# A four-layer attention kernel: sums one step behind the scores, PSUM laid out per stage, and the first query chunk started early

## The chip, the cores and the metric

The kernel runs on one core of one Trainium2 chip. The metric is device time in microseconds (us) of one execution. The kernel before takes 5196.6 us, the median of two runs that lie between 5195.6 and 5197.61. "Granted clock" is the share of full TensorE clock that the chip allowed in a stretch of time.

## The reference, cut to what matters

There are four layers, A, B, A, B, on one sequence of 2048 tokens with 1024 features and 32 heads of 32. Both kinds add their result to x.

```python
def _A_ref(x, wqkv, w_phi, wo):                    # linear attention
    ...
    phi_q = concat([softmax(q @ w_phi), softmax(-(q @ w_phi))])   # features of queries
    phi_k = concat([softmax(k @ w_phi), softmax(-(k @ w_phi))])   # features of keys
    kv  = einsum("bhsf,bhsd->bhfd", phi_k, v)      # needs every key first
    z   = einsum("bhsf->bhf", phi_k)
    o   = (phi_q @ kv) / (phi_q @ z + 1e-6)
    return o @ wo

def _B_ref(x, wqkv, wo):                           # full attention
    ...
    p = softmax((q @ k.T) * Dh ** -0.5)
    return (p @ v) @ wo

x = x + _A_ref(_layernorm(x), A_wqkv, A_w_phi, A_wo)
x = x + _B_ref(_layernorm(x), B_wqkv, B_wo)
x = x + _A_ref(_layernorm(x), A_wqkv, A_w_phi, A_wo)
x = x + _B_ref(_layernorm(x), B_wqkv, B_wo)
```

Layer B has 32 x 2048 x 2048 scores, and each needs an exponential. Layer A has an obstacle in it: no query can be finished before all keys have been summed.

## The kernel before

Tokens are handled in four chunks of 512. The stages follow each other in this order. The first stage makes normalisation, values and key features of the first layer A. Then, twice: the projections to B (query features of A, its output projection, normalisation, keys and values of B, and B's queries for the first chunk), and the attention of B. The code calls the first pair of layers A and B "layer 0" and the second pair "layer 1", and so does this text.

Attention runs in steps, 1,024 in all. One step takes one group of four heads, 256 queries and 256 keys. It has 8 score matmuls, packed four at a time by rows of the array, two exponentials of 128x1024, and 16 sum matmuls, packed four at a time by columns. Half of the sums are with the values and half with ones, which gives the softmax denominators.

```python
def step(self, q, kv, g, half, kc, begin, end, acc, oT, first, last):
    n = 3 if mode[0] == "narrow" else 2
    ...  # two score tiles of two PSUM banks each, from a ring of n
    for k in range(2):
        for j in range(4):
            ...
            PE.matmul(tiles[j // 2][:, o:o + QH], lhsT=kv[rows, 0, ...],      # L496
                      rhs=q[rows, g, ...], start=True, stop=True,
                      tile_position=(32 * j, 0), skip_group_check=True)
    for i in range(2):
        e = T("E", [P, 2, 2, QH], BF16)
        SC.activation(out=e[:], in_=tiles[i][:]..., func=ACT.Exp, scale=SCALE)  # L505
        es.append(e)
    self.lag = (kv, g, half, kc, begin, end, acc, oT, first, last, es)

def finish(self):
    if self.lag is None:
        return
    kv, g, half, kc, begin, end, acc, oT, first, last, es = self.lag
    self.lag = None
    if begin:
        self.nd = psum.tile([P, C], F32, tag="ND", ...)       # one bank for the sums
    ...
                PE.matmul(nd[rows, part * QH:(part + 1) * QH],                # L527
                          lhsT=ones_bf[:, 0:32] if part else kv[:, 1, col:col + 32],
                          rhs=es[j // 2][:, j % 2, i, :], ...)
    ...  # at the end of a group: copy or add nd to acc, or divide into oT
```

Other work (projections of the next queries, output projection of the chunk before) is a generator; it is dealt out in pieces between a step's scores and its sums:

```python
for _ in b:                    # one attention step: scores and exponentials
    got = 0.0
    while alive and got < per:
        u, end = next(bg)      # one piece of background work, usually 8 matmuls
        got += u
        if end:
            break
    att.finish()               # the sums of the same step
```

PSUM has 8 banks of 2 KiB per partition (the Trainium skill, "PSUM — Partial Sum Buffer", Specifications; the layouts of both kernels are built to that number). The kernel before holds three two-bank tiles for scores, one bank for sums (ND) and one for background work (BG). When no attention runs, projections use the two-bank tiles, cut in two:

```python
t = psum.tile([P, 2 * C], F32, tag=f"S{2 - k}", name=f"wide{serial[0]}")
halves.extend([t[:, 0:C], t[:, C:2 * C]])
```

The softmax here doesn't subtract the row's maximum and nothing guards it: scores larger than these inputs give would overflow.

## Time and profile before

The stages are read from the timeline, from the first matmul of one to the first of the next:

| stage | us |
|---|---|
| first stage | 396 |
| layer 0, projections of the first chunk / of the three others | 144 / 386 |
| layer 0, attention of four query chunks | 1,779 |
| layer 0, last output projection and the next layer's keys | 105 |
| layer 1, projections | 530 |
| layer 1, attention | 1,816 |
| tail | 40 |

Attention is about 3,590 of 5,197 us. The page of the kernel before gives the whole-span shares of the engines, the granted clock in 40 slices in tenths, and the chain of work that ended last:

```profile
PE 3167.5 (61%) x29982; PEld 1346.2 (26%) x30208; DVE 1326.9 (26%) x1808; ACT 2160.7 (42%) x2353; POOL 276.9 (5%) x218
...
PEclk9777787755696588578557877855585567556555
...
PE 45%; ACT 21%; issue 18%; DVE 7%; POOL 1%; DMA 0%; another core or an unknown queue 0%; ACTq 0%; POOLq 0%; DVEq 0%; SPq 0%
```

No engine is near full, and the clock falls to half in the attention stages. The windows view of the kernel before shows two stretches of attention, one without and one with background work:

```profile
core 0: us, PE busy (x) PEld busy (x) DVE busy (x) ACT busy (x) POOL busy (x), PEclk, DMA share, GB/s
1100.00:1300.00 200.00, 108.33 (x1318) 45.22 (x1308) 17.91 (x19) 104.76 (x109) 0.00 (x0) 0.50 0.05 17
940.00:970.00 30.00, 20.92 (x275) 9.39 (x280) 6.33 (x8) 19.38 (x20) 0.00 (x0) 1.00 0.20 71
```

Without background work PE is busy 108 of 200 us and ACT 105 of 200, at a clock of 0.50. With background work the clock is 1.00, and the step takes 3.03 us instead of 3.67. Two engines at about half, neither of them waiting for anything else, are the picture of a serial loop: each works while the other waits. The timeline of the kernel before shows the loop (columns: start, length, engine, line, operation, tiles, shape, and in brackets the idle time before it and what ended it):

```profile
983.72 1.02 ACT L505 ACTIVATE E_4820<-s_4810 128x1024 bf16<-128x1024 f32 x1 [1.73 <-PE s_4811 L496]
984.64 1.02 ACT L505 ACTIVATE E_4822<-s_4811 128x1024 bf16<-128x1024 f32 x1
984.80 0.40 PE L527 MATMUL nd_4763<-E_4820,kv_4177 128*32 128x256 bf16 x2 [1.17 <-ACT E_4820 L505]
985.71 0.40 PE L527 MATMUL nd_4763<-E_4822,kv_4177 128*32 128x256 bf16 x2 [0.52 <-ACT E_4822 L505]
...
986.88 0.42 PE L496 MATMUL s_4841<-q_2496,kv_4177 32*128 32x256 bf16 x2
987.39 1.02 ACT L505 ACTIVATE E_4850<-s_4840 128x1024 bf16<-128x1024 f32 x1 [1.73 <-PE s_4841 L496]
```

ACT starts the pair of exponentials at 983.72 and the next pair at 987.39: 3.67 us a step, of which it waits 1.73 for scores. PE waits 1.17 and 0.52 us for the exponentials. The sums wait for the exponentials of their own step, and the program has the next scores behind those sums: the lines show PE take them up in this order, the last sums at 985.71 and the next scores at 986.88.

The second thing to see is in the projections. The timeline of the kernel before, PE, in an output projection, one line for one group of 8 matmuls of 512 columns:

```profile
594.53 3.18 PE L156 MATMUL wide_2800<-c_531_2728,w_2640 128*128 128x512 bf16 x8
598.49 1.89 PE L156 MATMUL wide_2800<-c_531_2728,w_2640 128*128 128x512 bf16 x8 [0.78 <-DVE x_1968 L408]
600.21 1.89 PE L156 MATMUL bg_2819<-c_531_2728,w_2640 128*128 128x512 bf16 x8
```

Two groups share the tile "wide_2800", one in each half. The second waits until DVE has emptied the first half, although it writes the other bank.

### The profile page before, as it was taken

What the parts mean: (1) busy time and instruction counts of PE and PEld (TensorE: products, weight loads), DVE (VectorE), ACT (ScalarE), POOL (GpSimd) and SP (SyncE); (2) the same over time, 40 slices, a digit from 0 to 9 for tenths busy, and PEclk for the clock granted to TensorE, in tenths of its full rate; (3) what the DMA queues carried; (4) which work ended last, traced back from release to release, by engine and by line L of the source; (5) the groups of instructions that cost most, each with busy time, mean ns of one, the idle gap of its engine ahead of it and who ended that gap; (6) DMA issues with size and microseconds to landing.
All of it is one profiled execution on the core that took longest, in us unless ns stands there. A gap on an engine that the chain in (4) does not pass through costs nothing.

```text
span 5197.0 us, 68008 instructions
## 1 busy us (share of the span) xinstructions
PE 3167.5 (61%) x29982; PEld 1346.2 (26%) x30208; DVE 1326.9 (26%) x1808; ACT 2160.7 (42%) x2353; POOL 276.9 (5%) x218
## 2 busy tenths in 40 slices
PE   4656666655676577567555766755565566556555
PEld 2232222222232233223222222222222222222222
DVE  3454444100123023123115444310021011111101
ACT  1010000455566566556541000155565555555553
POOL 1221000000000000000001000000000000000000
PEclk9777787755696588578557877855585567556555
DMA  5223333200021021011002333400011001000000
GB/s 156 93 77 122 113 120 119 94 17 17 25 94 41 17 84 50 25 60 50 25 12 90 123 117 117 138 28 22 17 54 45 17 25 54 29 17 25 26 17 9
DMA packets 221416, 309.59 MB, mean 60 GB/s; under 512 B 41920, under 2 KB 189376, under 8 KB 213440
## 3 DMA queue, kind: packets, MB, share of 16 engines
q1 hardware_dynamic: 221120, 305.23, 17.8%
q8 instruction: 236, 3.87, 0.3%
q14 instruction: 60, 0.49, 0.0%
HBM read 236.52 MB, written 60.29 MB: 57 GB/s over the span
## 4 chain that ended last, share of the span: by engine, by line
PE 45%; ACT 21%; issue 18%; DVE 7%; POOL 1%; DMA 0%; another core or an unknown queue 0%; ACTq 0%; POOLq 0%; DVEq 0%; SPq 0%
PE nd_7976 L527 0%; PE nd_28185 L527 0%; PE nd_36665 L527 0%; PE nd_12464 L527 0%; PE nd_39829 L527 0%; PE nd_40078 L527 0%; PE nd_26208 L527 0%; PE nd_6989 L527 0%; PE nd_40816 L527 0%; PE nd_20937 L527 0%; PE nd_19701 L527 0%; PE nd_15758 L527 0%; PE nd_39088 L527 0%; PE nd_38322 L527 0%; PE nd_36173 L527 0%
## 5 line engine op out<-in xcount | busy, mean ns | idle before, releaser
L527 PEld LDWEIGHTS <-ones 128*32 128x32 bf16 x8192 | 417.8, 118 | 24.7
L183 PEld LDWEIGHTS <-ones 128*128 128x128 bf16 x128 | 12.9, 103 | 168.6 <-issue 167.2
L379 PEld LDWEIGHTS <-Rsel 128*128 128x128 bf16 x128 | 17.0, 133 | 143.7 <-issue 143.7
L179 POOL TENSOR_TENSOR sq_9474<-c_1591_9471 128x512 bf16<-128x512 bf16 x1 | 1.4, 1354 | 606.5 <-DVE c_1591_9471 L173 606.5
L188 ACT ACTIVATE f_3978<-wide_3945,eps 128x512 f32<-128x512 f32 x1 | 0.7, 687 | 71.1 <-PE wide_3945 L183 71.1
L188 ACT ACTIVATE f_23660<-wide_23616,eps 128x512 f32<-128x512 f32 x1 | 0.7, 687 | 69.6 <-PE wide_23616 L183 69.6
L188 ACT ACTIVATE f_23132<-bg_23099,eps 128x512 f32<-128x512 f32 x1 | 0.7, 687 | 69.5 <-PE bg_23099 L183 69.5
L188 ACT ACTIVATE f_24187<-wide_24154,eps 128x512 f32<-128x512 f32 x1 | 0.7, 687 | 69.5 <-PE wide_24154 L183 69.5
L188 ACT ACTIVATE f_22524<-wide_22480,eps 128x512 f32<-128x512 f32 x1 | 0.7, 687 | 69.3 <-PE wide_22480 L183 69.3
L188 ACT ACTIVATE f_2923<-bg_2890,eps 128x512 f32<-128x512 f32 x1 | 0.7, 687 | 69.2 <-PE bg_2890 L183 69.2
L188 ACT ACTIVATE f_3451<-wide_3407,eps 128x512 f32<-128x512 f32 x1 | 0.7, 687 | 68.5 <-PE wide_3407 L183 68.5
L188 ACT ACTIVATE f_2315<-wide_2271,eps 128x512 f32<-128x512 f32 x1 | 0.7, 687 | 67.9 <-PE wide_2271 L183 67.9
L344 ACT ACTIVATE ea_22805<-f_22803 128x512 bf16<-128x512 f32 x2 | 1.1, 620 | 58.2 <-DVE f_22803 L341 58.2
L344 ACT ACTIVATE ea_2596<-f_2594 128x512 bf16<-128x512 f32 x2 | 1.1, 621 | 57.5 <-DVE f_2594 L341 57.5
L156 PEld LDWEIGHTS <-c_109_666 128*128 128x128 bf16 x128 | 14.0, 110 | 38.7 <-issue 28.5
L156 PEld LDWEIGHTS <-c_266_1434 128*128 128x128 bf16 x128 | 13.7, 107 | 36.4 <-issue 25.4
L156 PEld LDWEIGHTS <-c_34_316 128*128 128x128 bf16 x128 | 14.2, 111 | 34.2 <-issue 24.2
L156 PEld LDWEIGHTS <-c_3416_21758 128*128 128x128 bf16 x128 | 13.3, 104 | 32.9 <-issue 21.1
L156 PEld LDWEIGHTS <-c_188_1054 128*128 128x128 bf16 x128 | 13.1, 104 | 32.5 <-issue 20.2
L344 ACT ACTIVATE ea_3124<-f_3122 128x512 bf16<-128x512 f32 x2 | 1.1, 620 | 42.2 <-DVE f_3122 L341 42.2
L505 ACT ACTIVATE E_4173<-s_4163 128x1024 bf16<-128x1024 f32 x1 | 1.0, 1023 | 41.4 <-PE s_4163 L496 41.4
L527 PEld LDWEIGHTS <-kv_7235 128*32 128x32 bf16 x128 | 8.2, 116 | 38.5 <-issue 37.3
(11593 smaller groups left out, 10645.7 us busy)
## 6 DMA issues: line engine op xcount, KB each, us to landing
w_301<-in_A_wqkv_dram SPq DMA_DIRECT2D x1, 1024.0 KB, 7.2
w_303<-in_A_wqkv_dram SPq DMA_DIRECT2D x1, 1024.0 KB, 8.4
x_d_72<-x_162 SPq DMA_DIRECT2D x1, 1024.0 KB, 4.2
x_d_73<-x_291 SPq DMA_DIRECT2D x1, 1024.0 KB, 4.5
w_404<-wpk_d SPq DMA_DIRECT2D x1, 1024.0 KB, 6.5
xa_d_76<-c_34_316 SPq DMA_DIRECT2D x1, 1024.0 KB, 3.8
w_444<-wpk_d SPq DMA_DIRECT2D x1, 1024.0 KB, 6.6
w_651<-in_A_wqkv_dram SPq DMA_DIRECT2D x1, 1024.0 KB, 6.6
```

Of the source, the lines that this page charges most:

```text
L156: PE.matmul(ps, lhsT=lhsT(po), rhs=rhs(po), start=(po == 0), stop=(po == G - 1))
L179: (DVE if fast and po % 2 else POOL).tensor_tensor(out=sq[:], in0=xc[:, po, :], in1=xc[:, po, :], op=ALU.mult)
L183: PE.matmul(ps, lhsT=ones_bf[:], rhs=sq[:], start=(po == 0), stop=(po == G - 1))
L188: SC.activation(out=lnv[:], in_=ps, func=ACT.Ln, scale=1.0 / D, bias=eps_t[:])
L344: SC.activation(out=e[:, s, :], in_=pq[:], func=ACT.Exp, scale=1.0 - 2.0 * s)
L379: PE.matmul(ps, lhsT=Rsel[:, g, s, :], rhs=ab[:], start=True, stop=True)
L505: SC.activation(out=e[:], in_=tiles[i][:].rearrange("p (j k q) -> p j k q", k=2, q=QH), func=ACT.Exp, scale=SCALE,)
L527: PE.matmul(nd[rows, part * QH:(part + 1) * QH], lhsT=ones_bf[:, 0:32] if part else kv[:, 1, col:col + 32], rhs=es[j // 2][:, j % 2, i, :] ...
```

## The change

The change has four parts.

1. The sums run one step behind. Scores and exponentials of step n+1 are issued before the sums of step n.
2. PSUM is laid out anew per stage: 8 single banks for projections alone ("wide"); 2 score tiles, 3 background banks and ND in a middle stage ("mid"); 3 score tiles, one background bank and ND in the rest of attention ("narrow"). No projection uses half of a two-bank tile.
3. The first query chunk attends to each key chunk as soon as that is made, beside the projections of the next chunk. Its partial sums wait in SBUF (`acc`).
4. In the first stage ACT takes squares and evictions, exponentials of key features read PSUM directly, POOL no longer squares, and the normalisation of the next chunk is dealt between the projections of this one.

The diff, cut to its core:

```diff
-        w=4, c8=3, x=2, q=2, kv=2, st=2, E=5, ea=8, acc=4, f=6, r=3, sq=4, nd=2,
+        w=3, c8=3, x=2, q=2, kv=2, st=2, E=6, ea=8, acc=4, f=6, r=3, sq=4, nd=2,
 ...
+    LAYOUT = {"wide": (0, 8), "mid": (2, 3), "narrow": (3, 1)}   # score tiles, other banks
 ...
+    def ps512(dt=F32):
+        PS["ring"] += 1
+        return ps_tile(f"BG{PS['ring'] % PS['nb']}", C if dt == F32 else P, dt)[:]
 ...                                                   # normalisation
-            (DVE if fast and po % 2 else POOL).tensor_tensor(out=sq[:], ...)
+            if fast:
+                SC.activation(out=sq[:], in_=xc[:, po, :], func=ACT.Square)
+            else:
+                DVE.tensor_tensor(out=sq[:], in0=xc[:, po, :], in1=xc[:, po, :], op=ALU.mult)
 ...                                                   # key features
-                pk = T("f", [P, C], F32)
-                DVE.tensor_scalar(out=pk[:], in0=ps, scalar1=rcol[:, t:t + 1], ...)
+                if fast:
+                    for s in range(2):
+                        col = (res["ncol"] if s else rcol)[:, t:t + 1]
+                        SC.activation(out=e[:, s, :], in_=ps, func=ACT.Exp, scale=col)
+                else:
+                    ...                               # as before
 ...                                                   # attention
-            self.lag = (kv, g, half, kc, begin, end, acc, oT, first, last, es)
+            self.lag.append((kv, g, half, kc, begin, end, acc, oT, first, last, es))
 ...
-                att.finish()
+                if len(att.lag) > 1:
+                    att.finish()
+        while att.lag:
+            att.finish()
 ...                                                   # order of the stages
+            drain(to_b(0, x))                          # projections of chunk 0
+            set_mode("mid")
+            for c in range(1, NCH):
+                x = load_x(c)
+                together(
+                    att, [att.block(qs[0], 4 * c - 4, 4 * c, acc, None, c == 1, False)],
+                    to_b(c, x), 8,
+                )
             set_mode("narrow")
 ...
+                block = (
+                    att.block(qs[i], 0, S // P, None, oT, True, True) if i
+                    else att.block(qs[0], 12, 16, acc, oT, False, True)
+                )
+                together(att, [block], chain(*work), 8 if i == 0 else 4)
```

## The prediction

> **What bounds the kernel now.** The two attention stages. The timeline shows exponentials of scores from 928 to 2705 us and from 3341 to 5156 us: 1,024 steps in 3,590 of 5,197 us. The rest is projections, linear attention and normalisation in series. A step is a serial loop: 8 score matmuls, two exponentials, 16 sum matmuls that wait for them, then the next scores. Timeline at half clock: second exponential's result to next scores' weight load 0.97 us, scores to exponential 0.71, two exponentials to their result 1.99: 3.67 us. Where a background projection runs, the clock is full and the step is 3.03 us, so background work is already hidden. The windows show ACT 53% busy, PE 54%, granted clock 0.50 without background work, 0.97 with it: neither engine is the limit, the loop is. The Trainium skill ("TensorE: Matmul & The Clock Gate", The HAM clock gate) has just these two states; the trace has only 0.5 and 1.0.
>
> **What the change does.** (1) Sums of step n run behind the scores of n+1, so the loop spans two steps: 3.67/2 = 1.83 us even at half clock. ACT then binds: exponentials of 128x1024 start 0.92 us apart, 1.84 us a step. (The skill, "ScalarE: Activation LUTs", What ACT_TABLE_LOAD costs, gives 186 ns + 0.833 per element, overlapping by 93, so 0.95; the trace decides.) With background work PE needs 0.54 (sums) + 0.33 (scores) + 0.97 (four 512-column matmuls) = 1.84: a tie, so about 1.95. Key-feature steps add 1.2 us of exponentials per two steps: 2.4.
> (2) In the middle stage only two score buffers remain, so scores wait for both earlier exponentials: 1.99 + 0.5 = 2.5 us, 3.1 with feature exponentials. 32 of its 62 background pieces overlap; the rest is drained alone. The reciprocal chain (9 us on DVE) stalls PE there.
> (3) One bank per wide tile removes the 0.78 us wait of every second group on its neighbour's eviction.
> (4) In the first stage ACT takes evictions and squares; the DVE chain per key tile falls from 4.3 us to about 2.4, and normalisation overlaps. Without POOL, centring falls from 1.45 to 0.6 us (undisturbed pitch against the rest).
>
> **Sum (us, estimates from these durations).** First stage 262 (was 396). Each layer: first chunk 120 (148), three middle chunks 3 x 159 (32 steps ~94, drained ~61, reload ~4), last quarter of query chunk one 72. Query chunks two to four: 265 each in layer 0 (78 steps with background, 50 at 1.86), 243 in layer 1 (430 to 457 before). Last projection and keys of layer 0: 75 (105); tail 36. Total about 3,240; I say 3,250. Nearly all is critical; the matmul count is unchanged.
>
> **What would show it.** Steps of 1.84 to 2.0 us in narrow stages, ACT over 90% busy there where no keys are made; 2.5 us in the middle stages; the clock no longer at 0.5 for 400 us, or of no consequence; no wait on wide-tile evictions; the chain of waits dominated by ACT, "issue" small.
>
> **What would make it wrong.** Switching between row- and column-packed matmuls costs PE more, so that background steps take 2.2: +100 us. Clock oscillating: background steps near 3 us for a while. Evictions of the single background bank or the sums' bank queued behind DVE work. Middle steps at 3 us: +90. Weights arriving late with three buffers.
>
> Faster by over 2%: 0.98; within 2%: 0.01; slower: 0.01. Time 3,250 us, range 3,090 to 3,470.

## The result, and the profile after

The changed kernel takes 3168.66 us, the median of two runs (3167.23 and 3170.1). The ratio is 0.6098, with a 95% interval of 0.6071 to 0.6124. Each ratio in this document compares the fast runs of one kernel with those of the kernel before in the same rounds, so it is not quite the ratio of the medians quoted beside it. The time lies in the predicted range, 81 us below the point.

| stage (us) | before | predicted | after |
|---|---|---|---|
| first stage | 396 | 262 | 249 |
| layer 0, projections of the first chunk | 144 | 120 | 117 |
| layer 0, three other chunks (after: with three quarters of query chunk one) | 386 | 477 | 460 |
| layer 0, query chunk one (after: its last quarter) | 460 | 72 | 68 |
| layer 0, query chunks two to four | 1,318 | 795 | 809 |
| layer 0, last projection and keys | 105 | 75 | 70 |
| layer 1, projections (after: with three quarters of query chunk one) | 530 | 597 | 578 |
| layer 1, attention (after: the rest of it) | 1,816 | 801 | 791 |
| tail | 40 | 36 | 26 |

The prediction read some stages of the kernel before at slightly other places, so it has 148 where this table has 144.

The same three lines of the page, for the kernel after:

```profile
PE 2578.0 (81%) x30208; PEld 1123.8 (35%) x30208; DVE 1276.4 (40%) x1931; ACT 2129.9 (67%) x2433; POOL 95.7 (3%) x88
...
PEclk8897978887999998999999897879799999999999
...
PE 47%; ACT 28%; DVE 14%; issue 6%; DMA 3%; SPq 1%; ACTq 0%; DVEq 0%; POOLq 0%
```

ACT does about as much work as before (2,130 against 2,161 us), in much less time. "Issue" in the chain falls from 18% to 6%. The windows view of the kernel after shows one stretch of the last attention stage and the two halves of one middle chunk, first with attention and then with the rest of the projections drained alone:

```profile
core 0: us, PE busy (x) PEld busy (x) DVE busy (x) ACT busy (x) POOL busy (x), PEclk, DMA share, GB/s
2950.00:3136.00 186.00, 149.10 (x2463) 67.44 (x2463) 42.22 (x63) 186.00 (x205) 0.00 (x0) 1.00 0.10 34
367.00:458.00 91.00, 71.87 (x852) 27.72 (x850) 39.98 (x56) 68.64 (x80) 0.00 (x0) 0.79 0.16 52
458.00:519.00 61.00, 53.07 (x244) 23.26 (x243) 27.51 (x46) 2.26 (x4) 0.00 (x0) 0.89 0.57 189
```

In the attention stage ACT is busy 186.00 of 186 us: it is now the limit, where it stood at 52% before. The clock is 1.00, where it was 0.50. The timeline of the kernel after shows the loop opened up:

```profile
3099.94 1.39 ACT L523 ACTIVATE E_40974<-S_6443_40964 128x1024 bf16<-128x1024 f32 x1
3100.86 1.38 ACT L523 ACTIVATE E_40976<-S_6444_40965 128x1024 bf16<-128x1024 f32 x1
3101.01 0.28 PE L514 MATMUL S_6447_40994<-q_33266,kv_40168 32*128 32x256 bf16 x2
...
3101.70 0.29 PE L541 MATMUL ND_40947<-E_40974,kv_40168 128*32 128x256 bf16 x2
3101.78 1.39 ACT L523 ACTIVATE E_41004<-S_6447_40994 128x1024 bf16<-128x1024 f32 x1
3102.30 0.29 PE L541 MATMUL ND_40947<-E_40976,kv_40168 128*32 128x256 bf16 x2 [0.31 <-ACT E_40976 L523]
```

The scores S_6447 of the next step run at 3101.01, before the sums that use E_40974 at 3101.70. Exponentials now start 0.92 us apart without a gap, so a step takes 1.84 us. Note that an exponential's length reads 1.39 us here and 1.02 before. The pitch of their starts, 0.92, is the cost; in a queue that is never empty the lengths overlap.

### The profile page after: what moved, and what is told of

It reads as the page before. It is cut to its first block, busy times and chain, and to the rows that moved or that the text cites. A ratio compares the mean times of both kernels' runs of the same rounds, so it can differ in the third digit from the quotient of the medians.

```text
span 3168.3 us, 68293 instructions
## 1 busy us (share of the span) xinstructions
PE 2578.0 (81%) x30208; PEld 1123.8 (35%) x30208; DVE 1276.4 (40%) x1931; ACT 2129.9 (67%) x2433; POOL 95.7 (3%) x88
## 4 chain that ended last, share of the span: by engine, by line
PE 47%; ACT 28%; DVE 14%; issue 6%; DMA 3%; SPq 1%; ACTq 0%; DVEq 0%; POOLq 0%
SPq L766 1%; DMA v_d<-st_5681 0%; DMA v_d<-st_24626 0%; DMA v_d<-st_4111 0%; DMA w_506<-wpk_d 0%; DMA w_1992<-wpq_d 0%; DMA w_245<-in_A_wqkv_dram 0%; DMA w_10216<-wpk_d 0%; DMA wpk_d<-st_492 0%; PE ND_14215 L541 0%; SPq L737 0%; DVE c_2904_18189 L175 0%; DVE c_2317_14246 L175 0%; DVE c_3634_22833 L175 0%; DVE c_3907_24490 L175 0%
## 5 line engine op out<-in xcount | busy, mean ns | idle before, releaser
L541 PEld LDWEIGHTS <-ones 128*32 128x32 bf16 x8192 | 275.6, 99 | 5.9
L188 PEld LDWEIGHTS <-ones 128*128 128x128 bf16 x128 | 12.7, 101 | 113.0 <-issue 111.6
L523 ACT ACTIVATE E_23157<-S_3685_23147 128x1024 bf16<-128x1024 f32 x1 | 1.0, 1026 | 46.1 <-PE S_3686_23148 L514 46.1
L523 ACT ACTIVATE E_2642<-S_482_2632 128x1024 bf16<-128x1024 f32 x1 | 1.0, 1024 | 46.0 <-PE S_483_2633 L514 46.0
L158 PEld LDWEIGHTS <-c_5_187 128*128 128x128 bf16 x128 | 13.4, 106 | 43.3 <-DMA w_506<-wpk_d 22.3
L523 ACT ACTIVATE E_27871<-S_4470_27861 128x1024 bf16<-128x1024 f32 x1 | 1.0, 1024 | 33.5 <-PE S_4471_27862 L514 33.5
L523 ACT ACTIVATE E_7356<-S_1267_7346 128x1024 bf16<-128x1024 f32 x1 | 1.0, 1024 | 33.0 <-PE S_1268_7347 L514 33.0
L523 ACT ACTIVATE E_24727<-S_3946_24717 128x1024 bf16<-128x1024 f32 x1 | 1.0, 1024 | 32.7 <-PE S_3947_24718 L514 32.7
L523 ACT ACTIVATE E_26297<-S_4207_26287 128x1024 bf16<-128x1024 f32 x1 | 1.0, 1024 | 32.5 <-PE S_4208_26288 L514 32.5
L523 ACT ACTIVATE E_5782<-S_1004_5772 128x1024 bf16<-128x1024 f32 x1 | 1.0, 1025 | 31.9 <-PE S_1005_5773 L514 31.9
L523 ACT ACTIVATE E_4212<-S_743_4202 128x1024 bf16<-128x1024 f32 x1 | 1.0, 1025 | 31.4 <-PE S_744_4203 L514 31.4
L158 PEld LDWEIGHTS <-ones 128*128 128x128 bf16 x128 | 12.1, 98 | 24.6 <-issue 10.8
## 6 DMA issues: line engine op xcount, KB each, us to landing
xa_d_73<-c_5_187 SPq DMA_DIRECT2D x1, 1024.0 KB, 10.3
```

The costliest lines, as they stand in the source:

```text
L158: PE.matmul(ps, lhsT=lhsT(po), rhs=rhs(po), start=(po == 0), stop=(po == G - 1))
L188: PE.matmul(ps, lhsT=ones_bf[:], rhs=sq[:], start=(po == 0), stop=(po == G - 1))
L523: SC.activation(out=e[:], in_=tiles[i][:].rearrange("p (j k q) -> p j k q", k=2, q=QH), func=ACT.Exp, scale=SCALE,)
L541: PE.matmul(nd[rows, part * QH:(part + 1) * QH], lhsT=ones_bf[:, 0:32] if part else kv[:, 1, col:col + 32], rhs=es[j // 2][:, j % 2, i, :] ...
```

## The experiments

Twelve kernels were run. All gave correct results, the two with added work too. "Step" below is the time from one step's first exponential to the next step's; medians are over one attention stage.

### 1. The changed kernel without the lag

```diff
-                if len(att.lag) > 1:
+                if att.lag:
                     att.finish()
```

> The changed kernel with its sums run in the same step again, nothing else undone. Theory (the lag breaks a serial loop): steps in the narrow stages go back to 3.0 to 3.7 us, query chunks two to four to 430 to 455 us each, the total to about 4,540 us (4,350 to 4,700). Rival (the new buffers, banks and overlap made most of the gain): below 3,600 us.

Measured: 4562.89 us (4562.76 and 4563.03), ratio to the kernel before 0.8782. The step is back to a median of 3.67 us in nearly every stage, the middle one too, and 3.03 us where background work runs. The windows view of this kernel in an attention stage without background work reads as it did before the change:

```profile
4250.00:4450.00 200.00, 107.46 (x1298) 44.99 (x1298) 19.71 (x21) 106.06 (x110) 0.00 (x0) 0.50 0.05 17
```

One line is worth 4562.89 - 3168.66 = 1,394 us. The theory holds. Part of this comes with the clock, which is 0.50 in this window and 1.00 in the kernel after. Without the lag a step takes 3.03 us even at full clock, with the lag 1.83: at least 1.2 us of the 1.84 us a step are the lag's own, and up to 0.64 us (3.67 - 3.03) go with the clock.

### 2. The kernel before with the lag alone

```diff
-        ... E=5, ...
+        ... E=6, ...
-            self.lag = None
+            self.lag = []
 ...
-            self.lag = (kv, g, half, kc, begin, end, acc, oT, first, last, es)
+            self.lag.append((kv, g, half, kc, begin, end, acc, oT, first, last, es))
 ...
-                att.finish()
+                if len(att.lag) > 1:
+                    att.finish()
+        while att.lag:
+            att.finish()
```

> The kernel before with the lag alone (and one more exponential buffer, which it needs). Theory: attention stages fall from 3,590 us to about 2,000, total about 3,610 us (3,550 to 3,750). Rival (the lag works only together with the other parts): above 4,200 us.

Measured: 3610.67 us (3609.77 and 3611.57), ratio 0.6949, granted clock 0.903. The step is 1.83 us everywhere. The lag alone takes 1,586 of the 2,028 us, without a new layout and without the early start.

### 3. Two score tiles in all of attention

```diff
-    LAYOUT = {"wide": (0, 8), "mid": (2, 3), "narrow": (3, 1)}
+    LAYOUT = {"wide": (0, 8), "mid": (2, 3), "narrow": (2, 3)}
```

> The changed kernel with two instead of three score buffers in the narrow stages, the banks given to background work. Theory (scores must be able to start while the step before is still in its second exponential): 2.5 us a step as in the middle stage, total about 3,720 us (3,600 to 3,800). Rival (the lag alone hides everything): below 3,250 us.

Measured: 3618.98 us, ratio 0.6965. The step is 2.50 us, or 2.39 where the clock is full. The timeline shows the loop that remains with two tiles:

```profile
3400.44 0.61 PE L514 MATMUL S<-q,kv 32*128 32x256 bf16 x6 [0.52 <-ACT E L523]
3400.95 1.94 ACT L523 ACTIVATE E<-S 128x1024 bf16<-128x1024 f32 x2 [0.56 <-PE S L514]
...
3403.45 1.94 ACT L523 ACTIVATE E<-S 128x1024 bf16<-128x1024 f32 x2 [0.56 <-PE S L514]
```

Scores wait for exponentials to free their tile, and exponentials wait 0.56 us for scores. 3403.45 - 3400.95 = 2.50 us. The third score tile is therefore worth about 0.67 us a step, and this is the price that the middle stage pays for its three background banks.

### 4. The kernel before with single banks alone

The `ps512` and layout code of the change is put into the kernel before; nothing else is moved.

```diff
-            t = psum.tile([P, 2 * C], F32, tag=f"S{2 - k}", name=f"wide{serial[0]}")
-            halves.extend([t[:, 0:C], t[:, C:2 * C]])
-        return halves.pop(0)
 ...
+    LAYOUT = {"wide": (0, 8), "mid": (2, 3), "narrow": (3, 1)}
 ...
+        return ps_tile(f"BG{PS['ring'] % PS['nb']}", C if dt == F32 else P, dt)[:]
```

> The kernel before with one bank for each wide tile and nothing else. Theory: the 0.78 us waits of every second group on its neighbour's eviction go, about 80 us for each layer's projections and 15 in the first stage: about 5,020 us (4,970 to 5,080). Rival (those waits are replaced by others): above 5,140 us.

Measured: 4923.28 us, ratio 0.9476. It gains about 273 us, where about 175 were expected (5,020 us). The chunks of projections come 102.3 us apart, where they were 128, and the first stage is 43 us shorter, where 15 were expected. The rest of the gain, some 230 us where 160 were expected, lies in the projections of both layers. The guess had been worked out from the 0.78 us wait of one place. In the first stage of the kernel before, the same kind of wait is much longer (columns: who waited, for what, us in total, times, longest):

```profile
PE wide_1681 L156 <- DVE f_1690 L249: 7.7, 1, 7.7
PE wide_1282 L156 <- DVE f_1291 L249: 7.6, 1, 7.6
PE wide_603 L280 <- DVE kva_300 L288: 7.0, 1, 7.0
```

The eviction that the second half waits for stands in DVE's queue behind the feature sums and their divisions. The waits of PE's projections for the key eviction L249 alone are 50.2 us in 12 times in that stage. With single banks no projection waits for it any more; 8.5 us of waits for it are left elsewhere. The first two lines of the first stage's list are now:

```profile
PE BG L184 <- POOL sq L180: 74.2, 32, 16.1
PE BG L281 <- DVE ea L265: 16.5, 8, 3.3
```

Part of the gain is given back: the waits for POOL's squares, 34.7 us in the kernel before, are now 74.2. In the three later chunks of layer 0, PE's waits summed over the list fall from 124 to 70 us. That is 54 of the 80 us or so which these chunks gain. The rest is in PE's busy time, 261 us before (540.8 to 928 us) and 234 now (473 to 779 us) for the same matmuls, while the mean granted clock rises from 0.79 to 0.85. The guess had counted no gain from the clock.

### 5. The first query chunk attends after all projections

```diff
-            set_mode("mid")
             for c in range(1, NCH):
-                x = load_x(c)
-                together(att, [att.block(qs[0], 4 * c - 4, 4 * c, acc, ...)], to_b(c, x), 8)
+                drain(to_b(c, load_x(c)))
             set_mode("narrow")
 ...
-                    else att.block(qs[0], 12, 16, acc, oT, False, True)
+                    else att.block(qs[0], 0, S // P, None, oT, True, True)
```

> The changed kernel without the early attention of query chunk one: all four chunks are projected first, then chunk one attends to all keys in the narrow stage. Theory (steps in the middle stage cost 2.9 us instead of 1.84, and half of the projections is drained alone, so little is hidden): three projections of 104 us and a block of 240 us against 528 us now, so plus 24 us a layer, about 3,216 us (3,190 to 3,250). Rival (the intent: 96 steps a layer vanish behind projections): plus 177 us a layer, about 3,520 us.

Measured: 3187.51 us (3185.14 to 3188.22, 4 runs), ratio 0.6136: only 19 us slower than the change, at the lower edge of what was expected and far from the rival's 3,520. The stages say why. Alone, three chunks take 3 x 99 = 297 us and the whole of query chunk one then takes about 243, together 540 us. In the changed kernel the three middle chunks and the last quarter take 366.7 to 894.9, 528 us. The overlap saves some ten us a layer. The early start is right in intent, but a step in the middle stage takes 2.9 us on average (median 2.50) instead of 1.89, and nearly half of the projections (30 of 62 pieces, 61 of the 153 us of each chunk) is left over and drained alone. Which of the two costs more is not separated here; experiment 9 takes up the second, and three score tiles in the middle stage were not tried.

### 6. The first stage as before

```diff
-        drain(ln_gen(xs[0], res, True))
+        drain(ln_gen(xs[0], res))
 ...
-            main = ak_gen(c, xs[c], sl, True, res, fold_first if c == 0 else None)
+            main = ak_gen(c, xs[c], sl, False, res, fold_first if c == 0 else None)
 ...
-                drain(merge(main, ln_gen(xs[c + 1], nres, True), 4))
+                drain(main)
+                drain(ln_gen(xs[c + 1], nres))
```

> The changed kernel with the first stage as before: evictions and squares off ACT, normalisation not merged with the chunk before. Theory: the DVE chain per key tile is 4.3 us again and normalisation is exposed, plus about 100 us, 3,270 us (3,240 to 3,300). Rival (the banks made the first stage faster): plus less than 40 us.

Measured: 3263.06 us (3261.02 to 3266.63), ratio 0.6283: 94 us slower, all of it before the first query features, which DVE now takes up at 349 us rather than 252. The share of ACT and that of the merged normalisation were not separated. POOL does not square in this experiment either, so part of the first stage's gain is still in it. By first matmuls, the first stage takes 396 us in the kernel before, 353 with single banks alone (experiment 4), 346 here and 249 in the kernel after.

What taking POOL out does is read from the groups of one line, centring on DVE, in the first stage before and after (count, shortest/median/longest in ns, first and last start):

```profile
L173 DVE TENSOR_TENSOR c_109_666<-x_291,f_664 x8: 684/1522/1528, 131.8 to 140.2; 128x512 bf16<-128x512 bf16 x8
```

```profile
L175 DVE TENSOR_TENSOR c_132_816<-x_704,f_772 x8: 681/682/691, 118.0 to 122.2; 128x512 bf16<-128x512 bf16 x8
```

The same subtraction took 1.52 us beside POOL's squares and takes 0.68 without them. That POOL is the cause is shown by two runs: the median is 1.52 us in the first stage of experiment 4, where POOL still squares, and 0.69 in that of experiment 6, where DVE squares and nothing is merged. The Trainium skill ("GPSIMD Engine Reference", Specifications) says that the two engines share their SBUF interfaces and contend where the DVE instruction has two SBUF inputs. This one has two, and the trace agrees.

### 7. Every score matmul twice

```diff
-            for k in range(2):
+            for k in (0, 1, 0, 1):
```

> The changed kernel with the score matmuls of each step run twice (same result), 0.22 us more of PE a step. Theory (ACT bounds steps without background, PE ties with it where there is background): steps without background stay at 1.83 us; some 360 background steps and the 192 middle steps take 0.2 more: plus about 120 us, 3,290 us (3,230 to 3,340). Rival (PE or its waits bound every step): plus 225 us or more, above 3,390 us.

Measured: 3244.04 us (3242.59 to 3248.14), ratio 0.6243: 75 us more. Steps without background work stay at 1.83 us, at a clock of 1.00; PE has the room for eight more matmuls in them. Most steps with background work, 1.85 us before, grow to 2.0 to 2.1 us. The middle stages (early start and drained rest) take 42 of the 75 us: their steps go from a median of 2.50 to 2.6 to 2.9 us. So ACT bounds the light steps, and PE is so close to it in heavy steps that any addition shows.

### 8. Half an exponential more in each step

```diff
+                if i:
+                    SC.activation(out=e[:, 0, :, :], in_=tiles[i][:, 0:C]...,
+                                  func=ACT.Exp, scale=SCALE)
```

> The changed kernel with a third exponential of half a tile in each step (same values written again), about 0.5 us more of ACT. Theory (ACT bounds nearly every step): all of it shows, 1,024 times 0.5, about 3,680 us (3,600 to 3,730). Rival (PE bounds the steps with background): 300 us or less, below 3,480 us.

Measured: 3733.3 us (3732.44 to 3734.51), ratio 0.7182, just above the expected range. The median step in narrow stages is 2.46 us, with and without background work: 0.63 us more. In the timeline the third exponential, which overwrites what the second wrote, starts 0.03 us after the second has ended (3552.24 after 3552.21), while the first two overlap by 0.10. Over all 1,024 steps the mean is 565/1,024 = 0.55 us more, since heavy steps had some room on ACT. A step without background work thus pays for added ACT work in full, so ACT is its limit. The window in the last attention stage brings a surprise:

```profile
3450.00:3650.00 200.00, 161.63 (x1985) 63.94 (x1977) 36.09 (x56) 197.48 (x245) 0.00 (x0) 0.50 0.09 32
```

The clock has fallen to 0.50 although PE has the same matmuls to do, only at 2.46 us a step. It costs nothing here, since ACT is busy 197 of 200 us. Half the clock is thus of no consequence where ACT is the limit. In the kernel before it did lengthen the step, 3.67 us against 3.03 at full clock, because there PE's time was part of the loop.

### 9. Two background pieces in each middle step

In the changed kernel 61 us of each middle chunk are drained without attention beside them, while later attention is short of background work. The next runs try to gain that.

```diff
-    def together(att, blocks, bg, per):
+    def together(att, blocks, bg, per, pieces=1):
 ...                      # the dealing loop runs `pieces` times a step
-                    to_b(c, x), 8,
+                    to_b(c, x), 8, 2,
```

> The changed kernel with two background pieces after each step of the middle stages instead of one, so that all 62 pieces lie beside the 32 steps. Theory (the drained 61 us are PE's own work and could carry attention's waits): a middle chunk falls from 152 to about 112 us, six of them, total about 2,930 us (2,880 to 3,010). Rival (the middle stage is bound by DVE's chains and by scores waiting for two buffers whatever the order): less than 60 us gained, above 3,110 us.

Measured: 3044.56 us (3044.16 to 3047.42), ratio 0.5862. It is 124 us faster than the change, but the theory had expected 2,930. A middle chunk takes 132.7 us rather than 112. Its window:

```profile
366.50:499.30 132.80, 111.23 (x1100) 46.91 (x1098) 66.53 (x101) 71.64 (x83) 0.00 (x0) 0.91 0.39 127
```

PE is busy 111 of 133 us, ACT only 72. The theory had let attention hide behind the projections for nothing. But attention brings its own PE work of about 0.87 us a step (an estimate: 0.54 for sums and 0.33 for scores at full clock, from the timeline), 28 us in 32 steps. And it fills few of PE's waits: in experiment 5, where a chunk of projections takes 99 us alone, PE's waits in the list are 62 us for three chunks, 21 for one; here they are 21.5 us in the chunk, of which 5.4 are attention's own, for score tiles. The longest is for the result of the division of A's query features:

```profile
PE BG L403 <- DVE ab L395: 9.0, 1, 9.0
```

In the middle stage PE is the nearest limit, at 84% of the chunk, and its waits are the rest.

### 10. Background work dealt by its estimated time

```diff
-        yield 8, True                       # after the division of the query features
+        yield 50, True
-                yield 1, True               # broadcast
+                yield 3.2, True
-            yield 2, True
+            yield 3, True
 ...
+                credit += per
+                while even and credit > 0:
+                    credit -= next(bg, (1e9, True))[0]
 ...
-                    to_b(c, x), 8,
+                    to_b(c, x), 13.8, True,
```

> As the one with two pieces, but background work is dealt out by its estimated time, so that steps without background follow the reciprocal chain and more steps lie in normalisation. Theory: attention fills those waits, total at or below the two-piece version, about 2,910 us (2,860 to 3,000). Rival: the same as the two-piece version within 1%, the chains are not hidden because the engines run in order.

Measured: 3044.8 us (3044.06 to 3045.23), ratio 0.5861, the same as the run before. More even pieces gain nothing, as the rival said. One wait of PE stands out in the middle chunk of this kernel:

```profile
PE ND L542 <- DVE acc L552: 10.3, 1, 10.3
```

A wait of this kind was there in the changed kernel too. These are its lines of the timeline of the kernel after, DVE and PE:

```profile
395.65 3.34 DVE L389 RECIPROCAL f_3026<-f_3026 32x512 f32<-32x512 f32 x1
...
402.05 0.69 DVE L395 TENSOR_TENSOR ab_3028<-f_3027,ab_3028 32x512 bf16<-32x512 f32 x1
402.77 0.69 DVE L551 COPY acc_352_1979<-ND_2974 128x512 f32<-128x512 f32 x1
403.51 0.40 PE L541 MATMUL ND_3071<-E_3001,kv_2820 128*32 128x256 bf16 x2 [9.86 <-DVE acc_352_1979 L551]
```

PE does not wait for the result of the division of A's query features. It waits for the bank ND, whose eviction was issued behind that chain of eleven DVE instructions (L385 to L395). The Trainium skill ("TensorE: Matmul & The Clock Gate", Architectural detail: the array is 16× 32×32, not 1× 128×128) says that DVE's queue is strictly first in, first out; the trace agrees, with an eviction of 0.69 us held up for nearly ten. Experiment 10 did move the matmuls that need the chain's result away from it, but the wait of experiment 9 for that result (9.0 us) gave way to one for ND of about the same length (10.3).

### 11. The division cut into pieces

On top of experiment 10, the chain of DVE instructions gets points at which the attention may put its own between them.

```diff
+        yield 15, True
         DVE.reciprocal(out=t1[q0, :], in_=t1[q0, :])
+        yield 15, True
 ...
+        yield 10, True
         DVE.tensor_tensor(out=ab[q1, :], in0=t2[q0, :], in1=ab[q0, :], op=ALU.subtract)
         DVE.tensor_tensor(out=ab[q3, :], in0=t2[q2, :], in1=ab[q2, :], op=ALU.subtract)
-        yield 50, True
+        yield 10, True
```

> As the version dealt out by time, with the reciprocal chain on DVE cut into four pieces, so that the attention steps beside it put their evictions between them. Theory (the 11.9 us gap beside the chain is the copy out of the one sums bank, queued on DVE behind the chain: in the trace the sums wait 10.3 us for that copy once a chunk): no gap over 5 us, about 7 us less a chunk, six chunks, from 3,045 to about 3,000 us (2,980 to 3,025). Rival (PE had to wait for the chain's result anyway, attention there saves nothing): less than 10 us, above 3,034 us.

Measured: 3004.95 us (3003.24 to 3007.54, 4 runs), ratio 0.5784 with an interval of 0.5776 to 0.5792. Of the 40 us gained over experiment 10, about 31 are the wait for ND, if all six middle chunks are like the first, where it falls from 10.3 to 5.2 us; the rest was not traced. Cutting the chain in the changed kernel itself was not tried. This is the fastest version: it beats both kernels, and takes about 5% less than the change (the two ratios to the kernel before are 0.5784 and 0.6098, and their quotient is 0.949). The timeline of DVE shows the evictions inside the chain now, and the wait of PE is shorter in the list of waits:

```profile
386.38 0.69 DVE L555 COPY acc<-ND 128x512 f32<-128x512 f32 x1
386.99 3.33 DVE L390 RECIPROCAL f<-f 32x512 f32<-32x512 f32 x1
...
392.21 0.42 DVE L395 CAST ab<-f 32x512 bf16<-32x512 f32 x1
392.66 0.69 DVE L555 COPY acc<-ND 128x512 f32<-128x512 f32 x1
393.38 0.68 DVE L397 TENSOR_TENSOR ab<-f,ab 32x512 bf16<-32x512 f32 x1
```

```profile
PE ND L545 <- DVE acc L555: 5.2, 2, 3.2
```

### 12. A second bank for the sums

Also on top of experiment 10, in place of the cut chain:

```diff
-    LAYOUT = {"wide": (0, 8), "mid": (2, 3), "narrow": (3, 1)}
+    LAYOUT = {"wide": (0, 8, 1), "mid": (2, 2, 2), "narrow": (3, 1, 1)}
 ...
-                self.nd = ps_tile("ND", C)
+                self.nd = ps_tile(f"ND{PS['nring'] % PS['nn']}", C)
 ...                      # dealing by time as in experiment 10
```

> As the version dealt out by time, chain uncut, but the sums get a second bank in the middle stages, taken from background work (two banks left for it). Theory (it is the sums bank): the sums can go on for four steps of 2.5 us while DVE is in its chain, the gap falls below 5 us and the total to about 3,005 us (2,985 to 3,030). Rival: as above, or the missing background bank costs as much as is won, above 3,034 us.

Measured: 3029.78 us (3027.63 to 3032.12, 5 runs), ratio 0.5832, at the upper edge of the range. It gains 15 us, against 40 for the cut chain. In its middle chunk the wait is not gone:

```profile
PE ND L544 <- DVE acc L554: 5.5, 1, 5.5
```

A group of sums is two steps long in the middle stage, so a second bank lets PE run two steps further before it meets the same queue. The extra bank was taken from background work, and whether that costs something was not measured apart. A buffer puts such a wait off; cutting the chain left 5.2 us of it in the list, but no single wait over 3.2 us.

## Why the prediction was right

**The bound.** It said that a serial loop bounds the kernel, and no engine. Experiment 1 (the lag alone undone, +1,394 us) and experiment 2 (the lag alone done, -1,586 us) show this from both sides.

**The new step.** It said 1.83 to 1.84 us, by half of the loop's length or by two exponentials. Measured is 1.83. That both ways gave the same number is a coincidence: the measured steps run at full clock, so half of the half-clock loop was not what was tested. ACT as the new limit is shown by experiment 8, where a light step grows by 0.63 us with the added ACT work, and experiment 7, where added PE work leaves light steps as they were.

**Background steps.** It said 1.95, from a tie of PE and ACT; the median is 1.83 without and 1.85 with background work in layer 0. Instead the cost sits in few steps. In the plain projections of query chunk three, every eighth step or so takes 3.4 us, because the next projection waits for the one background bank; its eviction stands on DVE behind the division at the end of a group of heads. These are its lines of the kernel after, DVE and PE:

```profile
1181.86 1.75 DVE L564 RECIPROCAL rc_13318<-nd_13316 128x256 f32<-128x256 f32 x1
...
1183.99 0.68 DVE L472 TENSOR_TENSOR q_13000<-BG_2180_13295,r_13023 128x512 bf16<-128x512 f32 x1
1184.73 1.02 PE L158 MATMUL BG_2192_13371<-c_2139_13022,w_13028 128*128 128x512 bf16 x4 [1.46 <-DVE q_13000 L472]
```

Steps with normalisation beside them reach 7.9 us. Those with key features mostly alternate between 1.81 and 2.85, a mean of 2.33 for the predicted 2.4, and some take 5.5. The mean of query chunks two to four of layer 0 is 2.06 to 2.13 us, and they took 809 us together for a predicted 795. That the sum came so close was partly luck: 1.95 stood for a tie that costs almost nothing, and the waits that do cost stand only among the prediction's risks.

**The middle stage.** It said 2.5 us a step, 94 us for 32 steps and 61 us for the drained rest. Measured are 2.50 (median), 90 and 61 to 62. Experiment 3 shows that two score tiles make the 2.5 us, and experiment 5 that the early start, as dealt, is worth only 19 us. Experiment 9 wins 124 us with the same two tiles, so the drained rest is a large part of the reason.

**The chain of divisions.** It said that the chain "stalls PE there" for 9 us, and a wait of 9.9 us is there. The route was left open there, though "evictions of [...] the sums' bank queued behind DVE work" stands among the prediction's risks. It is this one, and not the obvious one: in the middle stage of the changed kernel PE waits for an eviction queued behind the chain, and not for the chain's result. The lines of the kernel after in experiment 10 show it. On the kernel of experiment 10, cutting the chain gains 40 us (experiment 11).

**Single banks.** "One bank per wide tile removes the 0.78 us wait of every second group on its neighbour's eviction" has the right mechanism: among PE's waits in the first chunk's projections of the kernel after (249 to 366 us) none is for such an eviction. What was mis-sized is the guess for experiment 4 that was made from it, 175 us for a measured 273: in the first stage these waits reach 7.7 us, because the eviction stands behind other DVE work, and in the projections the clock rose besides. The stage sums of the prediction did not suffer: none is off by more than 20 us.

**The first stage.** It said 262 and measured is 249. Experiment 6 shows 94 us of the 147 us gained to be ACT's part and the merged normalisation together. Centring took 0.68 us without POOL's squares, as it said (0.6 as a pitch).

**The clock.** It said "no longer at 0.5 for 400 us, or of no consequence". In the changed kernel it is 1.00 in the late attention stages. Experiment 8 shows the other branch: 0.50, and without consequence. What decides between the two is not settled (see the last section).

**The chain of waits.** "Dominated by ACT, 'issue' small" is half right. "Issue" fell to 6%, but PE's share is still 47% against ACT's 28%. The chain follows releases through the middle and projection stages as well, where PE is the busier engine. ACT's limit is plain in the windows of the attention stages, and hardly in that sum over the span.

The parts nearly add up: the lag alone 1,586, single banks alone 273, and, undone from the change, 94 for the first stage and 19 for the early start, together 1,972 of 2,028 us. They overlap and were measured from different ends, so the remainder of 56 us is not assigned.

## What to carry to other kernels

Where two engines are each half busy and no transfer is late, look for a serial loop between them, and issue the next step's first half before this step's second half; here that was worth 69% (experiment 1) to 78% (experiment 2) of the 2,028 us gained. Count the buffers that the overlap needs before sharing them out: with two score tiles in place of three the step took 2.50 us and not 1.83. Work that is meant to be hidden must also be dealt out in full: with half of it drained alone, the early start of attention gained 19 us, and with all of it dealt 143 (3187.51 - 3044.56). Look at what stands in an in-order queue ahead of a short eviction: cutting a chain of eleven instructions gained 40 us, a second buffer 15.

## What the Trainium skill lacked or had wrong

- "TensorE: Matmul & The Clock Gate" gives the clock gate two states, and the trace has only these, 0.5 and 1.0. It lacks how busy PE must be to keep the full clock. The same 24 packed matmuls a step held 1.00 at 1.83 us a step (the change), and 0.50 at 2.46 (experiment 8) and at 3.67 (before), while at 2.50 the window's mean was 0.53 (experiment 3). Its rule against idle gaps of more than about 3.4 us does not foretell this: PE's gaps in the step before the change were 1.17 us and less. It also tells of a clock that swings to and fro where PE is idle often and briefly; here the clock stayed at a mean of 0.50 through windows of 200 us.
- "ScalarE: Activation LUTs" gives a length and an overlap from which the pitch of a 128x1024 exponential comes out at 0.95 us (an estimate from that page); the trace has 0.92. It doesn't say that the recorded length grows in a full queue: 1.39 us in place of 1.02, at the same pitch of 0.92.
- "VectorE: DVE Perf Modes" tells how a reciprocal is computed, but no time for one. 32x512 in float32 took 3.34 us, where a multiplication of the same tile took 0.68.
- "GPSIMD Engine Reference" names the contention with DVE, but gives no size for it. A 128x512 subtraction with two SBUF inputs took 1.52 us beside POOL's squares and 0.68 without.
- No page that was consulted says what a strict queue does to a bank's eviction behind long work: 9.9 us of PE for an eviction of 0.69 us, and 1.46 us for one of 0.68.
